# A new static order for a fused attention and convolution kernel: other costs and a deadline in the planner, fewer filler matmuls, one PSUM bank per convolution, six slots for output rows

## The chip, the core and the metric

The kernel runs on one core of a Trainium2 chip. The core has five engines that run their own instruction streams and meet only at semaphores: TensorE (PE, with its weight loads shown as PEld), VectorE (DVE), ScalarE (ACT), GpSimd (POOL) and SyncE (SP). The metric is the device time of one execution in microseconds. Three runs of the kernel before gave 596.65, 601.78 and 606.09 us; the median is 601.78 us.

## What is computed

Two independent layers are computed on inputs of 2048 rows by 448 columns, and a gate mixes them.

```python
def _A_ref(x, wq, wk, wv, wo):                      # 16 query heads share one key/value head
    q = (x @ wq).reshape(B, S, H, Dh).transpose(0, 2, 1, 3)      # S = 2048, D = 448, H = 16, Dh = 28
    k = x @ wk
    v = x @ wv
    p = softmax(einsum("bhqd,bkd->bhqk", q, k) * Dh ** -0.5)
    return einsum("bhqk,bkd->bhqd", p, v).transpose(0, 2, 1, 3).reshape(B, S, H * Dh) @ wo

def _B_ref(u, A_re, A_im, B_re, B_im, C_re, C_im, log_dt, Dskip):
    K[d, l] = Re sum_n C[d, n] * exp(dt[d] * A[d, n] * l) * dt[d] * B[d, n]   # N = 256, l < 2048
    return causal_convolution(u, K) + u * Dskip                  # one kernel per channel d

g = sigmoid((x * gate_w).sum(-1))
out = g * _A_ref(x, ...) + (1 - g) * _B_ref(x, ...)
```

## The kernel before

**Attention.** The scores are made as 1024 tiles of 128 keys by 512 queries (four heads, sixteen key blocks, sixteen groups of queries and heads). A QK set makes three or two tiles in one go, by turns, into one half of the buffer `psS` (line 1077; operation `mm` in `qk`). One ACT instruction takes the exponential of the whole set into `expT` (line 1093). A PV step multiplies four such tiles by the values, two sets behind, and accumulates in `psB` (line 1102); a column of ones gives the softmax denominators. After 64 tiles `norm` copies `psB` to `acc` (line 992), sends the denominators through DRAM and back (POOL's DMAs `denT`, `R_scratch`, `rdenB`) and writes the normalised rows to `onT`, a ring of four slots. `outp` multiplies four slots by `Wo`, `fold` adds the result, times the gate, to the output tile `O`.

**State space part.** The channels go in fourteen blocks `c` of 32. `masters` (DVE) squares powers for two or four blocks at a time, `tables` (DVE) expands them to the two factors of the convolution kernel, `kgen` (PE, line 894: 16 operations of 8 matmuls) multiplies these, and POOL writes the result to `KP_scratch` in DRAM in nine DMAs. `tload` reads it back as Toeplitz tiles `T`: 112 loads of 1072 KB, issued by SP into a ring of five slots. `conv` (two for each block, each on four `T` tiles) runs 8 operations of 4 matmuls for a tile (line 938) into one PSUM bank, DVE scales the bank to `cst` (line 947), PE transposes it (`yt`, line 958) into a second bank, and DVE adds that to `O` (line 966).

**The order.** Nothing is decided at run time. `Prog.schedule` is a list scheduler over all operations: each has an assumed duration, a priority `pr` (smaller goes first) and dependencies, and the one that could start earliest on its engine is placed next. Two PSUM banks (`POOL = (7, 5)`) are handed out as locks to everything but attention. The result is a fixed instruction list for each engine; each engine works its list strictly in order.

**Fillers.** Afterwards `fill` (line 587) walks the PE list and puts matmuls of zeros (lines 599, 602, 606) into every stretch in which the plan leaves PE idle, for three quarters of that stretch at an assumed 54 ns each:

```python
room = start - e0 - (pg.SWITCH if m0 != o.mode else 0.0) - 40.0
n = int(room * self.FILL / 54.0)
```

A filler of the kind of line 606 is four matmuls on the four column groups of the array, one of line 599 is a single matmul on 32 rows. They add zeros to `psB`, or write a bank that is not in use yet.

## Time and profile before

| | us |
|---|---|
| median of three runs (lowest, highest) | 601.78 (596.65, 606.09) |
| the profiled execution, its own time | 595.78 |
| its span, first to last instruction | 594.0 |
| PE busy, with 11359 matmuls | 514.2 |
| PEld busy, with 11374 weight loads | 302.4 |
| ACT busy | 489.5 |
| DVE busy | 461.8 |
| POOL busy | 140.2 |
| mean granted TensorE clock, as a share of full | 0.902 |

The profile shows one execution. Its page gives busy times, a chain of waits that ended last, and groups of instructions with the idle time ahead of them and what ended it. "issue" there is time in which an engine waited for nothing that the profile shows. Views of a stretch (busy time, waits, DMA queues, the timeline) use microseconds from the start of the span. In the profile a matmul's bar is longer than the pitch at which matmuls follow each other, so busy PE time is not work at peak.

### The profile page before, as it was taken

How to read it: one execution, taken by the hardware profiler on the slowest of the kernel's cores; microseconds unless marked ns; L12 is line 12 of the kernel's file. 1: busy time of each engine (PE TensorE's matmuls, PEld its weight loads, DVE VectorE, ACT ScalarE, POOL GpSimd, SP SyncE). 2: the span in 40 equal slices, each digit the busy share in tenths (PEclk: the TensorE clock that was granted, in tenths of full speed). 3: DMA queues.
4: the chain of work that ended last, by engine and by line, in shares of the span. 5: the costliest groups of instructions: out<-in, count | busy, mean ns of one | idle time of the engine just before them, and what ended most of it. 6: DMA issues, size and time to landing. Idle time of an engine off the chain costs nothing.

```text
span 594.0 us, 24569 instructions
## 1 busy us (share of the span) xinstructions
PE 514.2 (87%) x11359; PEld 302.4 (51%) x11374; DVE 461.8 (78%) x870; ACT 489.5 (82%) x427; POOL 140.2 (24%) x281
## 2 busy tenths in 40 slices
PE   7689898789899998798798998988998988968892
PEld 6445464445545455445455545645554545645552
DVE  6959997969979999979689899889597989100122
ACT  3669979879789999879689999888797999977750
POOL 2000114104124424231131523131141432412000
PEclk9858959979889999979789999989798999987896
DMA  8822001965926948968947847978838836597974
GB/s 244 230 106 74 2 20 31 400 223 167 391 71 190 411 136 315 380 219 347 380 167 272 274 184 264 402 259 311 313 120 357 336 144 229 213 383 284 357 260 169
DMA packets 36302, 143.11 MB, mean 241 GB/s; under 512 B 8880, under 2 KB 19224, under 8 KB 21864
## 3 DMA queue, kind: packets, MB, share of 16 engines
q1 hardware_dynamic: 27320, 135.29, 61.4%
q0 software_dynamic: 8352, 6.09, 4.3%
q8 instruction: 89, 1.46, 1.0%
q10 hardware_dynamic: 528, 0.17, 0.2%
q14 instruction: 13, 0.11, 0.1%
HBM read 135.38 MB, written 5.74 MB: 238 GB/s over the span
## 4 chain that ended last, share of the span: by engine, by line
PE 48%; DVE 23%; ACT 15%; issue 8%; DMA 3%; POOL 0%; ACTq 0%; another core or an unknown queue 0%
ACT expT L1093 15%; PE psS L1077 14%; PE psB L1102 9%; PE psS L938 6%; PE psB L606 5%; PE psX L894 4%; PE psX L938 3%; DVE tab L855 3%; DVE tab L861 2%; DVE tmp L857 2%; DVE tab L857 2%; DVE tab L859 1%; PE psS L894 1%; PE psB L599 1%; DMA sz<-in_gate_w_dram 1%
## 5 line engine op out<-in xcount | busy, mean ns | idle before, releaser
L1093 ACT ACTIVATE expT<-psS 128x1536 bf16<-128x1536 f32 (+1 forms) x410 | 474.6, 1261 | 70.7 <-PE psS L1077 68.4
L1077 PE MATMUL psS<-qT,kT 29*128 29x512 bf16 x1024 | 176.1, 416 | 15.7 <-ACT expT L1093 8.6
L1102 PE MATMUL psB<-expT,vaug 128*32 128x512 bf16 x1024 | 110.6, 421 | 5.5 <-issue 3.0
L129 POOL DMA_DIRECT2D KP_scratch<-kstg x126 | 67.5, 543 | 118.1 <-DVE kstg L907 115.5
L606 PE MATMUL psB<-ident,zero 128*32 128x128 bf16 x2672 | 71.8, 236 | 10.6 <-issue 10.5
L1077 PEld LDWEIGHTS psS<-qT,kT 29*128 29x128 bf16 x1024 | 41.5, 93 | 73.4 <-ACT expT L1093 37.5
L938 PE MATMUL psS<-T,U 128*24 128x128 bf16 (+7 forms) x2048 | 58.4, 248 | 13.4 <-issue 13.0
L855 DVE TENSOR_TENSOR tab<-tab,mbf 128x256 bf16<-128x256 bf16 (+4 forms) x70 | 68.6, 982 | 1.0
L606 PEld LDWEIGHTS psB<-ident,zero 128*32 128x32 bf16 x2672 | 55.4, 105 | 26.5 <-issue 18.2
L1102 PEld LDWEIGHTS psB<-expT,vaug 128*32 128x32 bf16 x1024 | 26.7, 94 | 74.2 <-issue 69.2
L938 PEld LDWEIGHTS psS<-T,U 128*24 128x24 bf16 (+7 forms) x2048 | 49.8, 162 | 25.6 <-issue 22.9
L129 POOL DMA_DIRECT2D denT<-acc x60 | 30.3, 511 | 135.0 <-DVE acc L992 133.1
L947 DVE TENSOR_TENSOR cst<-psS,omq 128x512 bf16<-128x512 f32 x16 | 11.0, 688 | 46.7 <-PE psS L938 46.6
L938 PE MATMUL psX<-T,U 128*20 128x128 bf16 (+7 forms) x1536 | 41.4, 241 | 5.2 <-issue 4.5
L129 POOL DMA_DIRECT2D rdenB<-R_scratch x60 | 30.4, 513 | 60.0 <-DMA R_scratch<-denT 59.9
L894 PE MATMUL psX<-tab 128*32 128x64 bf16 x1024 | 40.1, 290 | 3.5 <-issue 3.2
L938 PEld LDWEIGHTS psX<-T,U 128*20 128x20 bf16 (+7 forms) x1536 | 36.0, 163 | 13.4 <-issue 11.1
L894 PEld LDWEIGHTS psX<-tab 128*32 128x32 bf16 x1024 | 29.4, 137 | 13.9 <-issue 11.5
L857 DVE TENSOR_TENSOR tmp<-tab,mbf 128x256 bf16<-128x256 bf16 (+3 forms) x56 | 36.3, 649 | 0.0
L599 PE MATMUL psB<-ident,zero 32*128 32x128 bf16 x401 | 32.6, 230 | 1.5 <-issue 1.5
L872 DVE TENSOR_TENSOR tab<-tab,tmp 128x4096 bf16<-128x4096 bf16 x14 | 32.0, 2289 | 0.2
L857 DVE TENSOR_TENSOR tab<-tab,mbf 128x4096 bf16<-128x4096 bf16 x14 | 32.0, 2284 | 0.0
(149 smaller groups left out, 571.5 us busy)
## 6 DMA issues: line engine op xcount, KB each, us to landing
T<-KP_scratch SPq DMA_DIRECT2D x112, 1072.0 KB, 9.7
rdenB<-R_scratch POOLq DMA_DIRECT2D x60, 64.0 KB, 5.2
U<-in_A_x_dram SPq DMA_DIRECT2D x3, 896.0 KB, 14.7
tab<-in_A_x_dram SPq DMA_DIRECT2D x4, 448.0 KB, 7.2
KP_scratch<-kstg POOLq DMA_DIRECT2D x112, 16.0 KB
SZ_scratch<-tab SPq DMA_DIRECT2D x1, 1344.0 KB, 6.1
out_dram<-O SPq DMA_DIRECT2D x3, 448.0 KB, 3.8
sz<-SZ_scratch SPq DMA_DIRECT2D x3, 384.0 KB, 10.4
```

What stands on the lines that cost most here:

```text
L129: return [e.dma_start(o, i, **kw) for o, i in pairs]
L599: r = e.matmul(t.v(0, P, bo, [[1, 128]]), self.zero.v(0, 32, 0, [[1, P]]), self.ident.v(0, 32, 0, [[1, P]]), start=not acc, stop=False, ti ...
L606: r = e.matmul(t.v(32 * j, 32, bo, [[1, 128]]), self.zero.v(0, P, 0, [[1, 32]]), self.ident.v(0, P, 0, [[1, P]]), start=not acc, stop=Fals ...
L855: vo(lambda e, dst=dst, src=src, mr=mr: e.tensor_tensor(dst, src, mr, ALU.mult), 2 * n, done + mk(lv), [kr, ki])
L857: vo(lambda e, src=src, mi=mi, w=w, tb=tb, to=to: e.tensor_tensor(tb.v(0, P, to, [[w * EW, 2], [EW, w], [1, EW]]), src, mi, ALU.mult), 2 * ...
L861: vo(lambda e, do=do, n=n, tb=tb, to=to: e.tensor_tensor(tab.v(0, P, do + BLK, [[1, n]]), tab.v(0, P, do + BLK, [[1, n]]), tb.v(0, P, to, ...
L872: vo(lambda e: e.tensor_tensor(tab.v(0, P, FM, [[64, 2], [EW, 32], [1, 64]]), tab.v(0, P, lo + 31 * EW, [[BLK, 2], [-EW, 32], [1, 64]]), r ...
L894: r = e.matmul(G.v(32 * g, 32, 64 * jj, [[1, 64]]), tab.v(0, P, lo + comp * BLK + 64 + o, [[EW, 32]]), tab.v(0, P, fo, [[mo - fo, 2], [EW, ...
L938: r = e.matmul(ps.v(32 * j, 32 - 2 * n, 128 * k, [[1, 128]]), self.U.v(0, P, 2 * n * D + 4 * gi + j, [[D, 32 - 2 * n]]), self.T.v(0, P, s ...
L1077: r = e.matmul(self.psS.v(0, P, 512 * (bo + k), [[1, 512]]), kT.v(32 * h, DH + 1, 128 * kt, [[1, 128]]), qT.v(32 * h, DH + 1, 512 * (i % 2 ...
L1093: pg.op("act", lambda e: e.activation(expT.v(0, P, 512 * es, [[1, n]]), self.psS.v(0, P, 512 * bo, [[1, n]]), AF.Exp, scale=SQ), 100 + n / ...
L1102: r = e.matmul(self.psB.v(32 * h, 32, 0, [[1, 512]]), vaug.v(0, P, 32 * kt, [[1, 32]]), expT.v(0, P, 512 * (t % RING), [[1, 512]]), start= ...
```

## The change

**Costs in the planner.** A QK set's exponential is assumed at 50 ns plus its elements, where it was 100 ns plus those. A convolution operation is assumed at 94 to 57 ns, by its place in the tile, where all had 58; a `kgen` operation at 226 for 235, a `yt` operation at 75 for 85. A new field `st` holds the time that an operation streams through the array.

**A deadline.** While a QK set is ready, the scheduler works out when it must start so that ACT does not run dry by the plan (`dead`), and places no other PE operation of lower priority that would end later than that.

**Priorities and banks.** Convolution operations go from priority 4 to 1.8, transposes from 3.5 to 1.3. The transposes write the convolution's own bank, so that one lock is held instead of two. `cst` has two slots, `onT` six. The masters are squared in place in `sz` (`mst` and `qst` are gone), so a reload of `sz` waits for the last of the block before.

**Fillers.** `fill` now counts, for eight windows of 3413 ns around each idle stretch, how much streaming the plan has in them, and fills only up to a share of 0.55, at an assumed pitch of 90 ns. The PE list has 1378 filler matmuls where it had 3140; all else keeps its count.

```diff
+    MARGIN = 120.0
...
+            dead, busy = None, free["act"]
+            for i in ready["act"]:
+                busy = max(busy, rt[i]) + ops[i].ns
+            for i in ready["pe"]:
+                o = ops[i]
+                if o.mode == "q":
+                    dead = max(rt[i], busy - o.lat - self.SEM_NS - o.ns - self.MARGIN)
...
+                    if e == "pe" and o.mode != "q" and dead is not None and o.pr > 0:
+                        g = r + (0.0 if o.mode == mode else self.SWITCH) + o.ns + self.SWITCH
+                        if g > dead:
+                            continue
...
+def on(i):
+    return i % NON
...
-    FILL = 0.75
+    FILL = 90.0
+    WIN = 3413.0
+    SHARE = 0.55
...
-        self.onT = sb("onT", 4 * 512, BF)
+        self.onT = sb("onT", NON * 512, BF)
...
-            room = start - e0 - (pg.SWITCH if m0 != o.mode else 0.0) - 40.0
-            n = int(room * self.FILL / 54.0)
-            if n > 0 and (opened or k < used):
+            room = start - e0 - (pg.SWITCH if m0 != o.mode else 0.0) - 60.0
+            need = 0.0
+            if room > self.FILL and (opened or k < used):
+                for w0 in range(8):
+                    a = e0 - self.WIN * w0 / 8.0
+                    got = sum(max(0.0, min(a + self.WIN, u + d) - max(a, u)) for u, d in act if a - 400.0 < u < a + self.WIN)
+                    need = max(need, self.SHARE * self.WIN - got)
+            n = int(min(room, need * self.FILL / 54.0) / self.FILL)
+            if n > 0:
                 mode = m0 if m0 in ("c", "f") else o.mode if o.mode in ("c", "f", "q") else "q"
                 out.append(filler(n, mode, 6 if opened else 5, opened))
+                act.append((e0, 54.0 * n))
...
-        mst, msq, msr, mbf = self.mst, self.msq, self.msr, self.mbf
+        mst, msq, msr, mbf = self.sz, self.msq, self.msr, self.mbf
...
-                pg.op("pe", lambda e, mm=mm, comp=comp: mm(e, comp), 235, mode="c", rd=keys,
+                pg.op("pe", lambda e, mm=mm, comp=comp: mm(e, comp), 226, mode="c", st=54.0, rd=keys,
...
-        ps, px = self.grp(), self.grp()
+        co, ck = 512 * (c % 2), ("cst", c % 2)
+        ps = self.grp()
+        for k in range(4):
+            self.tload(4 * c + k)
...
-                pg.op("pe", mm, 58, mode="c", rd=[("T", s)] + [("U", q) for q in range(3)],
-                      wr=[X] + (["cst"] if first else []), pr=4,
+                pg.op("pe", mm, (94, 92, 90, 82, 76, 70, 58, 57)[n], st=54.0, mode="c", rd=[("T", s)] + [("U", q) for q in range(3)],
+                      wr=[X] + ([ck] if first else []), pr=1.8,
                       lock=ps if first else None)
...
-            pg.op("pe", lambda e, k=k: yt(e, k), 85, mode="h", rd=["cst", "id"], wr=[Y], pr=3.5, lock=px if k == 0 else None)
+            pg.op("pe", lambda e, k=k: yt(e, k), 75, st=40.0, mode="h", rd=[ck, "id"], wr=[Y], pr=1.3)
...
-                                                AF.Exp, scale=SQ), 100 + n / 1.2, rd=bk, wr=ew, pr=0)
+                                                AF.Exp, scale=SQ), 50 + n / 1.2, rd=bk, wr=ew, pr=0)
```

**What it moves on PE: a convolution among attention.** This is PE's list before, between the third and the fourth `T` tile of the first convolution (`L938` with `T,U` is the convolution, `L1077` a QK set, `L1102` a PV step, `L606` fillers).

```order
L938 MATMUL psS<-T,U 18x128 x4
L606 MATMUL psB<-ident,zero 32x128 x4
L1077 MATMUL psS<-qT,kT 128x512 x2
L1102 MATMUL psB<-expT,vaug 32x512 x4
L606 MATMUL psB<-ident,zero 32x128 x36
L1077 MATMUL psS<-qT,kT 128x512 x3
L1102 MATMUL psB<-expT,vaug 32x512 x4
L938 MATMUL psS<-T,U 32x128 x4
```

This is the same place in the changed list, where `L963` is the convolution, `L1102` a QK set, `L1127` a PV step and `L624` fillers.

```order
L963 MATMUL psS<-T,U 18x128 x4
L624 MATMUL psB<-ident,zero 32x128 x20
L1102 MATMUL psS<-qT,kT 128x512 x3
L1127 MATMUL psB<-expT,vaug 32x512 x4
L963 MATMUL psS<-T,U 32x128 x4
```

Between the two tiles stand 20 filler matmuls where 40 stood, and one QK set where two stood.

**What it moves on PE: the end.** This is PE's list before, from the last PV step of all on (`L1042` is the last output product, `L1009` and `L1020` are the two steps of the last normalisation, `L938` is the third `T` tile of the last convolution but one).

```order
L1102 MATMUL psB<-expT,vaug 32x512 x4
L1042 MATMUL psS<-Wo,onT 128x448 x3
L938 MATMUL psX<-T,U 30x128 x4
L938 MATMUL psX<-T,U 28x128 x4
L938 MATMUL psX<-T,U 26x128 x4
L1009 MATMUL psS<-msq,acc 128x4 x4
L938 MATMUL psX<-T,U 24x128 x4
L938 MATMUL psX<-T,U 22x128 x4
L938 MATMUL psX<-T,U 20x128 x4
L938 MATMUL psX<-T,U 18x128 x4
```

This is the same place in the changed list (`L1067` is the last output product, `L1034` and `L1045` the two steps of the normalisation, `L963` the same third tile).

```order
L1127 MATMUL psB<-expT,vaug 32x512 x4
L1067 MATMUL psS<-Wo,onT 128x448 x6
L1034 MATMUL psS<-msq,acc 128x4 x4
L1067 MATMUL psS<-Wo,onT 128x448 x6
L963 MATMUL psX<-T,U 32x128 x4
L1045 MATMUL psS<-msq,rdenB 128x128 x4
L963 MATMUL psX<-T,U 30x128 x4
L963 MATMUL psX<-T,U 28x128 x4
L963 MATMUL psX<-T,U 26x128 x4
L963 MATMUL psX<-T,U 24x128 x4
L963 MATMUL psX<-T,U 22x128 x4
L963 MATMUL psX<-T,U 20x128 x4
```

The third tile now follows twelve output products and both steps of the normalisation, where it stood around the first step and after three products.

More of the change, by code (lines that the diff above doesn't have):

```diff
@@ L32 @@
 RING = 15
+NON = 6
 KW = 1088
@@ L70 @@
     __slots__ = ("i", "eng", "fn", "ns", "lat", "deps", "pr", "lock", "unlock", "slot", "ndma",
-                 "count", "vc", "end", "comm", "extra", "mode")
+                 "count", "vc", "end", "comm", "extra", "mode", "st")
 class Prog:
@@ L96, in op @@
         o.mode = mode
+        o.st = st or (ns if eng == "pe" else 0.0)
         o.lat = self.LAT[eng] if lat is None else lat
@@ L615, in filler @@
             return o.i
+        act = [(o.end - o.lat - o.ns, o.st) for o in (pg.ops[x] for x in order) if o.st > 0]
         for k, x in enumerate(order):
@@ L975, in outp @@
             pg.op("pe", lambda e, g=g: e.matmul(
-                px(), self.onT.v(0, P, g * 512 + 128 * tt, [[1, 128]]), self.Wo.v(0, P, g * D, [[1, D]]),
+                px(), self.onT.v(0, P, on(4 * qc + g) * 512 + 128 * tt, [[1, 128]]), self.Wo.v(0, P, g * D, [[1, D]]),
                 start=(g == 0), stop=(g == 3), tile_position=(0, 0), skip_group_check=True), 200,
-                rd=["Wo"] + [("on", gg) for gg in range(4)], wr=[X], pr=2, lock=G if g == 0 else None)
+                rd=["Wo"] + [("on", on(4 * qc + gg)) for gg in range(4)], wr=[X], pr=2, lock=G if g == 0 else None)
         self.fold(qc, tt, px, 0, D, [X], unlock=G)
```

54 lines of the change are left out of this document (24 added, 30 removed).

## Prediction

> **What bounds the kernel now.** I read the page first, then busy time by stretch, then who waited for whom in the long middle stretch. The page:
>
> ```profile
> span 594.0 us, 24569 instructions
> PE 514.2 (87%) x11359; PEld 302.4 (51%) x11374; DVE 461.8 (78%) x870; ACT 489.5 (82%) x427; POOL 140.2 (24%) x281
> q8 instruction: 89, 1.46, 1.0%
> L1093 ACT ACTIVATE expT<-psS 128x1536 bf16<-128x1536 f32 (+1 forms) x410 | 474.6, 1261 | 70.7 <-PE psS L1077 68.4
> ```
>
> The exponentials alone take 474.6 us, 0.4635 us for each of the 1024 tiles. They cannot overlap each other, so nothing below about 475 us plus a head and a tail is possible. ACT sat idle 70.7 us ahead of them, nearly all of it for a QK set. The chain of waits around 48 us shows the pace when nothing is missing: 21 in 24.06 us, 1.146 us each.
>
> ```profile
> 47.89 24.06 ACT expT L1093 x21
> ```
>
> By stretch (columns: length; busy time and instructions of PE, PEld, DVE, ACT, POOL; granted clock; DMA share; GB/s):
>
> ```profile
> 36.50:48.00 11.50, 11.50 (x137) 6.20 (x137) 8.35 (x12) 8.28 (x9) 0.00 (x0) 0.50 0.01 1
> 48.00:71.80 23.80, 20.21 (x408) 11.67 (x405) 23.16 (x78) 23.80 (x22) 2.14 (x4) 1.00 0.16 47
> 71.80:88.90 17.10, 16.90 (x267) 9.90 (x267) 16.86 (x33) 13.25 (x13) 2.54 (x5) 0.50 0.07 18
> 100.00:572.50 472.50, 419.12 (x9839) 241.76 (x9852) 370.88 (x673) 414.42 (x358) 127.63 (x244) 0.93 0.74 272
> 572.50:594.00 21.50, 10.29 (x254) 7.49 (x250) 6.94 (x12) 0.00 (x0) 0.00 (x0) 0.76 0.60 213
> ```
>
> The loss is in the middle: from 100 to 572.5 ACT is idle 472.50 - 414.42 = 58.1 us. Then 21.5 us of tail follow in which it has no work. In the middle, ACT waits for QK sets, and PE, which should make them, itself waits for nothing that the profile shows:
>
> ```profile
> ACT expT L1093 <- PE psS L1077: 56.1, 63, 3.2
> PE psS L938 <- issue: 13.0, 8, 3.3
> PE psB L606 <- issue: 10.5, 8, 2.2
> PE psX L894 <- issue: 3.2, 3, 1.7
> PE psX L938 <- issue: 3.2, 5, 2.0
> PE psB L1102 <- issue: 3.0, 2, 1.6
> PE psS L1077 <- issue: 2.5, 3, 2.0
> ```
>
> These six rows make 35.4 us in 29 waits, in convolutions, fillers, `kgen` and attention alike, so it is not the work at hand that stops PE. The DMA queues of that stretch show what does:
>
> ```profile
> q1 hardware_dynamic: 17087, 121.11, 67.9%
> q8 instruction: 76, 1.25, 1.0%
> ```
>
> The instruction queue moved 76 packets. Over the whole run it moved 89, and PE has 11359 + 11374 = 22733 instructions, 255 for each packet: the packets are PE's instructions, 256 at a time. 472.5 / 76 makes 6.2 us for a block of 256, while q1, with the `T` tiles, fills 68% of the engines. From 117.26 to 121.25 one block ran; the columns are start, length, engine, line, operation, count and the idle time ahead:
>
> ```profile
> 117.26 0.34 PE L606 MATMUL psB<-ident,zero 128*32 128x128 bf16 x9 [1.69 <-issue]
> 124.28 0.32 PE L938 MATMUL psS<-T,U 128*18 128x128 bf16 x3 [2.78 <-issue]
> ```
>
> PE came out of one issue wait at 117.26, and stood in the next from 121.5. Its matmuls in between, by group:
>
> ```profile
> L938 PE MATMUL psS<-T,U 128*32 128x128 bf16 (+7 forms) x60 | 1.7, 238 | 0.0
> L1077 PE MATMUL psS<-qT,kT 29*128 29x512 bf16 x10 | 1.6, 385 | 0.0
> L606 PE MATMUL psB<-ident,zero 128*32 128x128 bf16 x49 | 1.3, 220 | 1.7 <-issue 1.7
> L1102 PE MATMUL psB<-expT,vaug 128*32 128x512 bf16 x8 | 0.8, 390 | 0.0
> ```
>
> That is 127 matmuls and as many weight loads, one block. PE used it up in 4 us and got the next one 7.0 us after the last. **So PE starves for instructions wherever it runs through 256 of them in less than some 6 us**, and 49 of these 127 were fillers. What follows costs more:
>
> ```profile
> 117.26:124.28 7.02, 4.24 (x130) 2.71 (x130) 2.96 (x9) 4.62 (x4) 2.12 (x4) 0.91 1.04 377
> 124.28:129.84 5.56, 5.56 (x109) 3.02 (x109) 5.20 (x15) 3.31 (x3) 0.00 (x0) 0.50 0.68 241
> ```
>
> After the wait the clock is at half, and ACT is busy 3.31 of 5.56 us. Where blocks are spread evenly, none of this happens:
>
> ```profile
> 167.40:230.00 62.60, 60.10 (x1316) 32.30 (x1306) 59.60 (x104) 60.27 (x54) 23.65 (x45) 1.00 0.58 201
> ```
>
> 2622 instructions in 62.6 us are 6.1 us a block, the clock is full, and ACT loses 2.33 us, 3.7%.
>
> The Trainium skill, "Runtime: NRT & Kernel Launch", section "Instruction fetch mechanics", says that an engine's instructions come in blocks of 16 KiB, 256 instructions, over a DMA queue of its own, and that crossing a block is mostly hidden. The trace agrees on the block; on the hiding it does not, in this stretch.
>
> **The change, part by part.**
>
> *Fewer fillers.* In the middle stretch stand these:
>
> ```profile
> L606 PE MATMUL psB<-ident,zero 128*32 128x128 bf16 x2228 | 58.8, 231 | 10.6 <-issue 10.5
> L599 PE MATMUL psB<-ident,zero 32*128 32x128 bf16 x241 | 18.7, 220 | 1.5 <-issue 1.5
> ```
>
> That is 2469. The changed list has 959 from the same tile on (tile 128 of 1024), 1510 fewer; with their loads 3020 instructions, 11.8 blocks. 76 blocks become 64. At 6.2 us each these need 397 us, less than ACT's 414.4: on average fetching no longer binds. Locally it still can. I cut each PE list into pieces of 128 matmuls and gave each piece 0.4635 us for every QK tile in it, which is how long ACT takes over them. Where that is under the time of a fetch, the difference is lost. With 5.5 us for a fetch the list before loses 54 to 61 us, depending on where the cutting starts, and the changed one 12 to 17; with 6.2 it is 90 to 100, and 28 to 36. The measured 58.1 us is near the first pair. So ACT's idle time in the middle goes from 58.1 to between 12 and 36 by this count; the even stretch above, at 3.7%, would make it 17. I take 26, on the upper side, for the half clock that fewer fillers may bring and for `T` tiles that PE may now reach sooner. **That is -32**, with a best of -44 (3% left) and a worst of -12, if only the issue waits that now stand in fillers (10.5 and 1.5) go.
>
> *The deadline and the pitches.* They keep a QK set from queueing behind convolution work. In the even stretch, where nothing else disturbs, that is worth no more than its 2.33 us; over the middle 3.7% is 17 us at most, and it is inside the bounds above. The rule adds no wait on the chip, since it only chooses an order. Its cost would be convolutions that pile up for the end; the changed list has 224 convolution matmuls after the last QK set, against 192. I take nothing for that beyond the tail below.
>
> *Early part, 36 to 100 us.* ACT lost 3.2 us of 11.5 and 3.85 of 17.1 at half clock, and nothing at full clock. Fillers there go from 661 to 419 over the first 128 tiles. At half clock fewer of them stand ahead of a QK set, which saves up to half of these 7 us; if the half clock (22% lost) held over all 63.5 us, it would cost 7 more. I take +1, with 13 fewer of the fillers ahead of the first transposes in it.
>
> *The tail.* What ends the run is the last `T` load, which waits for the third tile of the last convolution but one:
>
> ```profile
> 574.51 1.05 PE L1009 MATMUL psS<-msq,acc 128*128 128x4 f32 x8
> 576.48 1.16 PE L1020 MATMUL psS<-msq,rdenB 128*128 128x128 f32 x8
> 576.01 5.89 DMA T<-KP_scratch
> 571.53 0.74 PE L1042 MATMUL psS<-Wo,onT 128*128 128x448 bf16 x3
> ```
>
> In the changed list nine more output products (0.22 us each by the last row) and the second step (1.16) stand ahead of that tile: 2.0 + 1.2 = 3.2 us, less the 0.4 that the tile's own operations now follow without a break. **+3**; between 0, if the products still run while PE waits for ACT, and 6 with one more issue wait.
>
> *The rest.* One bank for the convolution and its transposes, six slots in `onT`, two in `cst`: PE waited for none of these in the rows above, so I take 0. Squaring in place in `sz` delays three reloads on SP's queue behind the block before, with `T` loads queued behind them; they are placed where the plan has them ready, 0 to 10 us each if the plan is late, and I take 0.
>
> *The sum:* 594.0 - 32 + 1 + 3 = 566.0. The profiled execution's own time is 1.8 above its span, so 567.8. It was the fastest of all the runs shown, 6 us below their median. I expect less spread when the issue waits go, and **forecast 570 us**, with a range of its own from 554 to 586.
>
> **Rivals.**
>
> *The clock falls, slower.* Fillers keep the array busy; without them the clock could stay at half. For it: the stretches at half clock are among those with most fillers in the list, and there 661 go to 419. Against it:
>
> ```profile
> 345.50:353.00 7.50, 7.50 (x164) 4.44 (x164) 7.36 (x22) 7.50 (x8) 2.55 (x5) 1.00 0.43 163
> 68.40:71.80 3.40, 2.92 (x57) 2.06 (x53) 3.40 (x5) 3.40 (x4) 2.06 (x4) 1.00 0.03 2
> L599 PE MATMUL psB<-ident,zero 32*128 32x128 bf16 x30 | 2.0, 215 | 0.0
> L606 PE MATMUL psB<-ident,zero 128*32 128x128 bf16 x12 | 0.3, 219 | 0.0
> ```
>
> In the first window there is not one filler, and the clock stayed full. In the second 42 of 57 matmuls are fillers, there is no issue wait, and half clock followed at 71.8 all the same. Price: at half clock ACT loses 22% (13.25 busy of 17.10). With a share h of the middle at half clock it takes 414.4 / (1 - 0.03 - 0.225 h); today h is 0.14, by the clock of 0.93. At h = 0.38 the gain is gone, from 0.5 it is slower by 2%, and at 0.6 it is 414.4 / 0.835 = 496, 24 more than now: **about 624**. Chance 0.06; a half-way house, h about 0.35, at 590 to 602: 0.11.
>
> The Trainium skill, "TensorE: Matmul & The Clock Gate", section "Why this matters for your kernels", asks for no idle gap of PE over about 3 us to keep the clock. By that rule the changed kernel would keep it, and the issue waits alone lose it. The second window above disagrees: its clock fell without such a gap.
>
> *The fetch is not the cause.* If blocks are late for another reason, the issue waits (35.4) stay, and only the remaining 58.1 - 35.4 = 23 us can shrink, to the 17 of the even stretch: 594.0 - 6 + 4 + 1.8 = **594**. For it, fetches are only 1% of DMA time; against it, the wait after 117.26 came exactly at a block's end. Chance 0.10. The skill's "mostly hidden", above, is this case.
>
> *Another bound comes up.* DVE works 461.8 us, and `T` loads move 121 MB; PE faster by 5% may wait for either in its fixed order. If half of the 32 us is lost to that: **584**. Chance 0.11. The DMA share of 0.74 in the middle leaves a quarter, which speaks against more.
>
> **How the numbers follow.** The forecast holds 0.62, and the others 0.06, 0.11, 0.10 and 0.11 as said. About 2%, 12 us, is what a measurement of this kernel can tell from no change, so faster is below 589.7. All of the forecast, the last rival and a third of the fetch case lie there: 0.62 + 0.11 + 0.04 = 0.77. Slower is the clock rival, 0.05 of its 0.06; the rest, 0.18, is within 2%. The range runs from 552, the best of the middle and tail, to 597, which leaves out the clock's worse half and the forecast's ends.
>
> **What would show it.** In the changed profile the instruction queue has about 75 packets; PE's issue waits in the middle fall from 35 to below 15 us; the clock there rises from 0.93 to about 0.96; ACT's idle time ahead of its exponentials falls from 70.7 to about 40; the last stretch without ACT is near 24 us. I am wrong if the packets fall and the issue waits stay, or if both fall and the clock falls too.

## The result, and the profile after

The changed kernel takes **565.4 us** (median of four runs, 559.59 to 570.59), the kernel before 599.2 us in the runs beside it (591.75 to 606.09). The ratio is 0.948, with an interval from 0.932 to 0.965. This ratio and those of the table below leave out the runs that lie more than 1.5% above the fastest of their kernel, so they are not the quotients of the medians. The forecast was 570 us, with a range from 552 to 597.

The profiled execution of the changed kernel took 570.59 us, 5.2 above the median, at a mean clock of 0.860; that of the kernel before took 595.78, 3.4 below its median, at 0.902. So the profiles show a gain of 25.2 us where the medians show 33.8.

The page of the changed kernel:

```profile
span 568.8 us, 21055 instructions
PE 509.4 (90%) x9612; PEld 277.1 (49%) x9612; DVE 462.6 (81%) x870; ACT 486.5 (86%) x427; POOL 140.4 (25%) x281
q8 instruction: 75, 1.23, 0.8%
L1118 ACT ACTIVATE expT<-psS 128x1536 bf16<-128x1536 f32 (+1 forms) x410 | 471.6, 1291 | 41.5 <-PE psS L1102 35.0
```

75 packets of instructions instead of 89, and 41.5 us of idle time ahead of the exponentials instead of 70.7. By stretch (length; busy time and instructions of PE, PEld, DVE, ACT, POOL; granted clock; DMA share; GB/s), where the second ends with the last exponential:

```profile
36.50:100.00 63.50, 63.21 (x789) 30.91 (x788) 52.74 (x128) 56.77 (x50) 6.08 (x12) 0.57 0.08 23
100.00:540.34 440.34, 405.14 (x8322) 216.37 (x8326) 374.52 (x680) 411.08 (x359) 130.90 (x250) 0.92 0.78 287
540.34:568.80 28.46, 16.62 (x280) 11.52 (x268) 7.53 (x13) 0.00 (x1) 0.00 (x0) 0.62 0.60 221
```

The first of these stretches in the kernel before, which the prediction did not show:

```profile
36.50:100.00 63.50, 59.40 (x1019) 33.22 (x1020) 56.26 (x137) 56.43 (x51) 9.16 (x18) 0.78 0.10 25
```

In the middle ACT is idle 440.34 - 411.08 = 29.3 us (58.1 before). The tail is 28.46 us (21.50 before). The clock fell in the early stretch from 0.78 to 0.57, was 0.92 in the middle (0.93 before), and 0.62 in the tail (0.76 before). PE's waits in the middle for which the profile shows no releaser (total, times, longest):

```profile
PE psX L963 <- issue: 2.8, 4, 1.2
PE psX L917 <- issue: 2.7, 3, 1.4
PE psB L1127 <- issue: 1.9, 2, 1.3
PE psS L917 <- issue: 0.9, 1, 0.9
PE psS L963 <- issue: 0.6, 1, 0.6
PE psX L983 <- issue: 0.3, 1, 0.3
```

They make 9.2 us in 12 waits, all shorter than 1.5 us. Before there were 38.4 us in 32 waits (35.4 in the six rows that the prediction shows, and three small rows), up to 3.3 us long. What ACT waited for in the changed kernel's middle:

```profile
ACT expT L1118 <- PE psS L1102: 24.2, 41, 1.6
ACT expT L1118 <- PE psB L1127: 4.4, 2, 3.4
```

The second row is new: two exponentials waited for a PV step to free their slots in `expT`.

### The profile page after: what moved, and what is told of

It reads as the page before. It is cut to its first block, busy times and chain, and to the rows that moved or that the text cites. A ratio compares the mean times of both kernels' runs of the same rounds, so it can differ in the third digit from the quotient of the medians.

```text
span 568.8 us, 21055 instructions
## 1 busy us (share of the span) xinstructions
PE 509.4 (90%) x9612; PEld 277.1 (49%) x9612; DVE 462.6 (81%) x870; ACT 486.5 (86%) x427; POOL 140.4 (25%) x281
## 4 chain that ended last, share of the span: by engine, by line
PE 36%; ACT 22%; DVE 18%; DMA 17%; issue 3%; POOL 3%; ACTq 0%
ACT expT L1118 22%; PE psS L1102 11%; PE psB L1127 7%; DMA denT<-acc 6%; DMA T<-KP_scratch 4%; DMA rdenB<-R_scratch 3%; PE psB L617 2%; PE psB L624 2%; DMA R_scratch<-denT 2%; PE psX L963 2%; DVE tab L878 2%; DVE tab L880 2%; PE psS L917 2%; PE psX L917 2%; DVE tab L882 2%
## 5 line engine op out<-in xcount | busy, mean ns | idle before, releaser
L1118 ACT ACTIVATE expT<-psS 128x1536 bf16<-128x1536 f32 (+1 forms) x410 | 471.6, 1291 | 41.5 <-PE psS L1102 35.0
L1102 PE MATMUL psS<-qT,kT 29*128 29x512 bf16 x1024 | 183.4, 433 | 13.9 <-ACT expT L1118 10.0
L1127 PE MATMUL psB<-expT,vaug 128*32 128x512 bf16 x1024 | 113.8, 435 | 3.6 <-issue 1.9
L1102 PEld LDWEIGHTS psS<-qT,kT 29*128 29x128 bf16 x1024 | 42.4, 93 | 84.6 <-ACT expT L1118 48.7
L1127 PEld LDWEIGHTS psB<-expT,vaug 128*32 128x32 bf16 x1024 | 26.8, 95 | 72.5 <-issue 69.3
L963 PE MATMUL psX<-T,U 128*18 128x128 bf16 (+7 forms) x1920 | 54.9, 246 | 3.7 <-issue 2.8
L963 PEld LDWEIGHTS psX<-T,U 128*18 128x18 bf16 (+7 forms) x1920 | 46.6, 162 | 19.2 <-issue 15.3
L963 PE MATMUL psS<-T,U 128*32 128x128 bf16 (+7 forms) x1664 | 49.9, 246 | 6.2 <-DMA T<-KP_scratch 4.7
L963 PEld LDWEIGHTS psS<-T,U 128*26 128x26 bf16 (+7 forms) x1664 | 42.9, 161 | 17.5 <-issue 8.0
L917 PE MATMUL psX<-tab 128*32 128x64 bf16 x896 | 36.0, 289 | 2.8 <-issue 2.7
L624 PE MATMUL psB<-ident,zero 128*32 128x128 bf16 x1112 | 36.9, 259 | 0.1
L917 PE MATMUL psS<-tab 128*32 128x64 bf16 x896 | 34.7, 289 | 0.9 <-issue 0.9
L624 PEld LDWEIGHTS psB<-ident,zero 128*32 128x32 bf16 x1112 | 26.5, 114 | 12.9 <-issue 10.9
L917 PEld LDWEIGHTS psS<-tab 128*32 128x32 bf16 x896 | 26.1, 137 | 9.3 <-issue 7.2
## 6 DMA issues: line engine op xcount, KB each, us to landing
U<-in_A_x_dram SPq DMA_DIRECT2D x3, 896.0 KB, 15.9
```

The lines of the kernel that those rows point to most:

```text
L624: r = e.matmul(t.v(32 * j, 32, bo, [[1, 128]]), self.zero.v(0, P, 0, [[1, 32]]), self.ident.v(0, P, 0, [[1, P]]), start=not acc, stop=Fals ...
L917: r = e.matmul(G.v(32 * g, 32, 64 * jj, [[1, 64]]), tab.v(0, P, lo + comp * BLK + 64 + o, [[EW, 32]]), tab.v(0, P, fo, [[mo - fo, 2], [EW, ...
L963: r = e.matmul(ps.v(32 * j, 32 - 2 * n, 128 * k, [[1, 128]]), self.U.v(0, P, 2 * n * D + 4 * gi + j, [[D, 32 - 2 * n]]), self.T.v(0, P, s ...
L1102: r = e.matmul(self.psS.v(0, P, 512 * (bo + k), [[1, 512]]), kT.v(32 * h, DH + 1, 128 * kt, [[1, 128]]), qT.v(32 * h, DH + 1, 512 * (i % 2 ...
L1118: pg.op("act", lambda e: e.activation(expT.v(0, P, 512 * es, [[1, n]]), self.psS.v(0, P, 512 * bo, [[1, n]]), AF.Exp, scale=SQ), 50 + n / ...
L1127: r = e.matmul(self.psB.v(32 * h, 32, 0, [[1, 512]]), vaug.v(0, P, 32 * kt, [[1, 32]]), expT.v(0, P, 512 * (t % RING), [[1, 512]]), start= ...
```

## The experiments

The question was what the 29 us in the middle are made of (fewer instructions to fetch, less filler time on PE, or the new order), why the clock did not rise as forecast, and why the tail grew by 7 us and not by 3. "Middle" is from 100 us to the last exponential. "Issue" is the total of PE's issue waits there, "idle" ACT's idle time there, "clock" the granted clock there; the packets are those of the whole run, the tail is behind the last exponential. All but the first two columns come from each kernel's one profiled execution; those of e4 and e7 lay 8 and 17 us above their medians. Each ratio is taken to runs of the kernel before that were made beside that experiment; their medians lay between 597.9 and 602.1 us.

| kernel | median us | ratio to before, interval | packets | issue | idle | clock | tail |
|---|---|---|---|---|---|---|---|
| before | 599.2 | 1 | 89 | 38.4 | 58.1 | 0.93 | 21.5 |
| changed | 565.4 | 0.948 (0.932 to 0.965) | 75 | 9.2 | 29.3 | 0.92 | 28.5 |
| e1 before, new filler rule | 586.9 | 0.979 (0.970 to 0.988) | 81 | 25.1 | 49.7 | 0.92 | 21.7 |
| e2 changed, old filler rule | 571.6 | 0.958 (0.951 to 0.965) | 80 | 13.1 | 36.6 | 0.92 | 24.1 |
| e3 before, wide fillers | 572.9 | 0.961 (0.954 to 0.968) | 77 | 15.9 | 38.9 | 0.95 | 21.4 |
| e4 changed, no fillers behind tile 128 | 562.7 | 0.941 (0.933 to 0.949) | 67 | 0.8 | 27.5 | 0.86 | 29.2 |
| e5 before, no fillers behind tile 128 | 567.8 | 0.953 (0.947 to 0.959) | 69 | 2.8 | 34.1 | 0.85 | 21.8 |
| e6 before, light `T` loads | 548.2 | 0.919 (0.910 to 0.928) | 89 | 4.0 | 16.3 | 0.97 | 18.8 |
| e7 changed, old rule, wide fillers | 564.3 | 0.946 (0.938 to 0.955) | 72 | 8.3 | 33.8 | 0.91 | 30.7 |
| e8 changed, no deadline | 559.1 | no interval | 75 | 8.8 | 30.5 | 0.92 | 21.8 |
| e9 changed, last tile earlier | 565.1 | 0.943 (0.933 to 0.953) | 75 | 9.3 | 28.6 | 0.93 | 22.6 |
| e10 before, `T` loads in four pieces | 597.5 | 0.991 (0.985 to 0.997) | 89 | 30.7 | 60.0 | 0.93 | 21.0 |
| e11 changed, no deadline, old rule, wide | 554.8 | 0.926 (0.919 to 0.934) | 71 | 6.3 | 25.9 | 0.94 | 18.7 |
| e12 changed, light `T` loads | 535.7 | 0.898 (0.889 to 0.907) | 75 | 2.2 | 6.8 | 0.97 | 22.4 |

### e1: the new filler rule alone

```diff
-    FILL = 0.75
+    FILL = 90.0
+    WIN = 3413.0
+    SHARE = 0.55
...
(in fill, the counting of the changed kernel; kgen and conv with st=54.0, yt with st=40.0)
```

> The kernel before with only the new filler rule (windows of 3413 ns, share 0.55, pitch 90 ns); the old costs, priorities, banks, and no deadline. Fillers from tile 128 on: 1644, where the kernel before has 2479 and the changed one 959. Theory F (PE starves for instructions, 256 at a time): the list cut into pieces of 128 matmuls, 5.5 us for each piece and 0.4635 us for each QK tile in it, loses 28 to 34 us in the middle, where the list before loses 54 to 61 and the changed one 12 to 17 by the same count. So about half to two thirds of the whole gain of 34 us: 572 to 578 us against 599, PE's issue waits in the middle near 18 us (35.4 before, 9.2 in the changed kernel). Theory O (the gain is the new order: deadline, pitches, priorities): no gain, within 2% of 599, whatever the issue waits do.

Measured: 586.9 us, 2% less than before, where theory F had 572 to 578. Issue waits fell to 25.1 us, not as far as the 18 that F asked for. So the rule alone carries some two fifths of the gain (2.1 of 5.2%; with these intervals only a rough share), and F's count is too hopeful: 49.7 us idle where it had 28 to 34. A part of what is missing lies in the plan, that is, in the order and times that the scheduler works out before fillers go in: in the old plan this rule makes 1644 fillers behind tile 128, in the new plan 959.

### e2: the new plan with the old filler rule

```diff
-    FILL = 90.0
-    WIN = 3413.0
-    SHARE = 0.55
+    FILL = 0.75
...
-            n = int(min(room, need * self.FILL / 54.0) / self.FILL)
+            n = int(room * self.FILL / 54.0)
...
```

> The changed kernel with the old filler rule (three quarters of every idle stretch at 54 ns each); its costs, deadline, priorities and banks stay. Because the new costs leave less idle time in the plan, the old rule now makes 1417 fillers from tile 128 on (959 with the new rule, 2479 in the kernel before). Theory F: 19 to 26 us lost in the middle by the count with 5.5 us a piece, where the changed list has 12 to 17: 8 us slower than the changed kernel, 573 us, with issue waits near 15 us. Theory O: the same time as the changed kernel, 565 us. If the fillers hold the clock up (the clock theory), it is as fast or faster than the changed kernel, with a clock in the middle above 0.92.

Measured: 571.6 us, near the 573 of F, with 13.1 us of issue waits and the clock at 0.92, not above; the intervals of this kernel and of the changed one overlap. The old rule in the new plan makes 1417 fillers behind tile 128; in the old plan it made 2479. So **the new plan by itself takes away more fillers (1062) than the new rule does in the old plan (835)**. The likely reason is that a plan with longer assumed convolution operations has less idle time to fill, but costs, deadline, priorities and banks are new here together and were not told apart. The prediction counted these fillers as gone; it did not see that the plan, and not only the rule, removes them.

### e3: the same filler time in a quarter of the instructions

```diff
+                def one(c):
+                    mv = self.ident.v(0, P, 0, [[0, c], [1, P]]) if c > 1 else self.ident.v(0, P, 0, [[1, P]])
...
+                    for j in range(4):
+                        r = e.matmul(t.v(32 * j, 32, bo, [[1, P * c]]), self.zero.v(0, P, 0, [[1, 32]]), mv,
+                                     start=not acc, stop=False, tile_position=(0, 32 * j), skip_group_check=True)
...
-                for _ in range(n):
+                for _ in range(n // 4):
+                    r = one(4)
+                for _ in range(n % 4):
+                    r = one(1)
```

> The kernel before with the same filler time in a quarter of the instructions: every four fillers of 128 columns (four times 52 to 54 ns) become one of 512 columns. The order, the real work and the time that PE spends on fillers stay; 1315 filler matmuls are left from tile 128 on, where 2479 were. Theory F: issue waits in the middle fall from 35.4 to about 15 us, and by the count (17 to 31 us lost) the time falls by about 30 us, to 570, with the clock of the middle at 0.93 or above. If it is the time of the fillers on PE that counts, or their place ahead of QK sets, not the number of instructions: no change, within 2% of 599.

Measured: 572.9 us, with issue waits of 15.9 us. The middle of this kernel (the groups, and the stretch):

```profile
L1099 ACT ACTIVATE expT<-psS 128x1536 bf16<-128x1536 f32 x356 | 411.1, 1267 | 38.9 <-PE psS L1083 37.5
100.00:549.38 449.38, 416.90 (x8663) 220.06 (x8662) 368.96 (x668) 410.44 (x356) 125.54 (x240) 0.95 0.77 284
```

The order is that of the kernel before, PE spends about the same time on fillers in the middle (83.3 us of matmuls, 78.3 before), and 3.9% of the time is gone. So most of what these fillers cost is their number of instructions, not their time on PE nor their place in the list. That it is the fetching, e6 shows below: it keeps every filler and its weight load.

### e4 and e5: no fillers behind tile 128, in either order

```diff
...
-            if n > 0:
+            if n > 0 and done < 32:
...
             if pv is not None:
+                done += 1
                 opened = pv < 15
```

This is the edit of e4; `done` counts PV steps, of four tiles each. e5 puts the same condition into the kernel before.

> The changed kernel without any filler behind tile 128 of 1024 (959 fewer matmuls, 7.5 blocks of 256 instructions less). Theory F alone: 6 to 12 us lost in the middle instead of 12 to 17, issue waits below 4 us: about 560 us. The clock theory: without fillers the share h of the middle at half clock goes up; at half clock ACT lost 22% early on. The changed kernel has 0.92 there (h of 0.16); with h of 0.5 it would be 0.225 x 0.34 x 445 = 34 us slower, 599 us. Which of the two is larger tells what the fillers that are left are worth.

> The kernel before with no filler behind tile 128 of 1024; the old order and costs stay. From there on PE has as many instructions as the changed kernel without its fillers there had (59.7 blocks of 256), so the two differ by the order alone. Theory F (the block count sets the time, the order is worth little): ACT idle in the middle near 30 us (27.5 there, 58.1 before), issue waits below 5 us, about 565 us. Theory O (deadline, pitches and priorities carry the gain): no better than the kernel before with the new filler rule alone, 580 us or more, with ACT waiting for QK sets 45 us or more in the middle although the issue waits are gone.

Measured: 562.7 us in the new order (the changed kernel: 565.4; the intervals overlap), 567.8 in the old one. Both have the same number of instructions left there, and hardly an issue wait. The rows of the old order without fillers:

```profile
L1094 ACT ACTIVATE expT<-psS 128x1024 bf16<-128x1024 f32 x357 | 411.7, 1267 | 34.1 <-PE psS L1078 32.8
100.00:545.00 445.00, 402.84 (x7369) 200.08 (x7366) 368.86 (x670) 410.91 (x357) 126.63 (x242) 0.85 0.77 287
```

The middle of e4:

```profile
100.00:539.97 439.97, 404.22 (x7376) 198.14 (x7372) 374.85 (x681) 412.44 (x360) 131.50 (x251) 0.86 0.77 287
```

Two things follow. Taking out every filler of the middle gives 24.0 us of idle time (58.1 to 34.1) in the old order, with the clock down to 0.85; in this comparison the new order is worth 34.1 - 27.5 = 6.6 us of idle time. And the fillers that the changed kernel keeps there buy nothing that shows: without them the clock falls from 0.92 to 0.86, the issue waits go, and the idle time stays (29.3 and 27.5). The clock theory's 599 us did not come.

### e6 and e12: the same instructions, light T loads

```diff
-        pg.dma([(self.T.v(0, P, s * TW, [[1, TW]]),
-                 dram(self.KP, 4 * gi * KW, [[1, 64], [KH, 2], [1, TW]]))],
+        src = [[1, 64], [KH, 2], [1, TW]] if gi < NTR else [[1, 32], [1, TW]]
+        pg.dma([(self.T.v(0, P if gi < NTR else 32, s * TW, [[1, TW]]), dram(self.KP, 4 * gi * KW, src))],
```

This is the edit of e6; e12 makes the same one in the changed kernel. From the sixth load on only 32 of the 128 partitions of a tile are written, a quarter of the bytes. The convolutions then work on stale rows and the output is not the right one; every instruction is still there.

> The kernel before, all 2479 fillers kept, with the loads of T cut from the sixth on: 32 partitions of 128 are written, the others keep what the first five loads left (the convolutions behind them compute with stale rows). The order and the number of instructions stay. Theory F as the prediction put it (a block takes 6.2 us because T loads fill the DMA engines): issue waits in the middle fall from 35.4 us to below 10, and the time to 570 or below. If a block takes its time whatever the DMA engines carry, the issue waits stay above 25 us and the time above 588.

> The changed kernel with the loads of T cut from the sixth on to 32 partitions of 128 (the convolutions behind them compute with stale rows); its order and instructions stay. The kernel before, cut in the same way, took 548.2 us with 16.3 us of idle time on ACT in the middle. If the change gains by the fetch alone, nothing of its gain is left when the fetch is not short: 546 to 552 us, the same as the kernel before so cut, at 16 us of idle time in the middle, or a little slower by its tail and its clock. If the order gains by itself (5 us by the two runs without fillers): 540 us or below, 12 us idle or less. If the 29 us that the changed kernel still loses have another cause than the T loads, ACT stays idle for 25 us or more: 560 us.

Measured: 548.2 us for the kernel before so cut, 535.7 for the changed one. The kernel before, light loads (instruction queue of the whole run; the middle; its issue waits, all of them):

```profile
q8 instruction: 89, 1.46, 1.2%
100.00:527.36 427.36, 408.07 (x9856) 236.06 (x9853) 369.57 (x674) 411.01 (x359) 127.62 (x245) 0.97 0.40 100
PE psB L606 <- issue: 3.4, 4, 2.0
PE psX L894 <- issue: 0.6, 1, 0.6
```

Every filler is still there, 89 packets are fetched as before, in the same order; only the DMA share fell from 0.74 to 0.40, and 34 of 38 us of issue waits are gone. **A block of instructions is late because `T` loads fill the DMA engines.** The clock went up with it, from 0.93 to 0.97, without a filler added. The changed kernel, light loads:

```profile
L1118 ACT ACTIVATE expT<-psS 128x1024 bf16<-128x1024 f32 x357 | 404.6, 1402 | 6.8 <-PE psS L1102 4.1 <-PE psB L1127 2.5
100.00:510.64 410.64, 384.78 (x8305) 212.07 (x8314) 370.13 (x678) 403.80 (x357) 127.43 (x244) 0.97 0.40 103
```

6.8 us idle, where the kernel before has 16.3 under the same light loads and at the same clock. So 9.5 us of idle time go when the fetch is hardly short. They are not the order's alone, since the changed kernel also has fewer fillers and 2.2 us of issue waits for 4.0; between the two kernels without fillers, which differ by the order alone, it was 6.6. And 22.5 of the 29.3 us that the changed kernel still loses hang on the `T` loads, though its issue waits are only 9.2. How they divide was not tried: with light loads the clock is higher too, and other transfers land sooner (`rdenB` in 2.6 us by the median, where it took 5.5).

### e7, e8, e11: wide fillers and no deadline in the changed kernel

```diff
-                    if e == "pe" and o.mode != "q" and dead is not None and o.pr > 0:
+                    if e == "pe" and o.mode != "q" and dead is not None and o.pr > 99:
```

This is the edit of e8. e7 puts e3's wide fillers and the old rule into the changed kernel, e11 puts both together.

> The changed kernel with the old filler rule, every four of its fillers made one of 512 columns: the filler time of the run with the old rule in the changed kernel (571.6 us) in 715 filler matmuls from tile 128 on instead of 1417. Theory F: 65.3 blocks from there on, ACT idle in the middle 29 us as in the changed kernel (29.3 at 67.2 blocks) or less. With the clock held up by the filler time (0.85 instead of 0.57 between 36 and 100 us in the run with the old rule) the early stretch gains 3 us and the tail, at full clock, 4: about 558 us. If fillers as such cost PE time that QK sets need, it is no faster than 571.

> The changed kernel with the deadline taken out of the scheduler; costs, priorities, banks and the filler rule stay. It has 903 fillers from tile 128 on (959), 66.7 blocks for 67.2, so the fetch hardly differs. If the deadline is worth nothing beyond 2 us (the prediction): 563 to 567 us, ACT idle in the middle 27 to 32. If the deadline carries a part of the gain: 575 us or more, ACT waiting for QK sets 40 us or more in the middle, in waits that end with a convolution ahead of the QK set.

> The changed kernel without the deadline, with the old filler rule, and every four fillers made one of 512 columns: 64.9 blocks from tile 128 on, 160 convolution matmuls behind the last QK set (224). What the earlier runs showed apart, put together: the fetch as in the changed kernel (issue waits 8 us), a tail of 22 us instead of 28, and a clock of 0.9 or above. About 556 us, if the gains add up; 564, as with the wide fillers and the deadline, if the deadline's absence is worth nothing.

Measured: e7 564.3 us, no better than the changed kernel, though better than e2 with the same filler time in small pieces (571.6; the intervals just touch). The early stretch did not get the full clock back in its profiled execution (0.53), so the gain of 7 us forecast for clock and tail did not come. e8 559.1 us, below the 563 to 567 that were expected, but its runs go from 545.54 to 563.67, too wide for an interval; its quickest run had a mean clock of 0.937, its slowest 0.867. ACT's idle time in the middle, 30.5, is that of the changed kernel (29.3): in the middle the deadline is worth nothing that shows. In the tail it costs: without it 160 convolution matmuls stand behind the last QK set, with it 224. The tail is 21.8 us at a clock of 0.79 there, where e2, with the deadline and a clock of 0.78, has 24.1.

e11 takes **554.8 us** (551.58 to 558.01; 556 were expected), 0.926 of the kernel before, and 554.8 / 565.4 = 0.981 of the changed kernel's median. By its median it is the quickest version found that does all of the work; its interval just touches that of the changed kernel. Its tail and its middle:

```profile
534.08:552.81 18.73, 9.49 (x227) 7.02 (x225) 6.93 (x12) 0.00 (x0) 0.00 (x0) 0.88 0.60 221
L1114 ACT ACTIVATE expT<-psS 128x1536 bf16<-128x1536 f32 x358 | 409.4, 1315 | 25.9 <-PE psS L1098 19.5 <-PE psB L1123 4.2 <-PE psB L617 1.3
```

### e9: the third tile ahead of half of the products

```diff
-                      wr=[X] + ([ck] if first else []), pr=1.8,
+                      wr=[X] + ([ck] if first else []), pr=0.3 if c >= 26 else 1.8,
```

> The changed kernel with the last two convolutions at priority 0.3 (1.8): on PE the third tile of the last convolution but one now follows six of the twelve output products and only the first of the two normalisation steps, and the fourth tile follows it; nothing else moves. If the last T load, which waits for that tile, ends the run (the prediction's step for the tail): the tail behind the last exponential falls from 28.4 us by 3 us or more. If the tail is PE's own work at half clock, one after the other (the products took 0.41 us each there, 0.22 before): the tail stays at 27 to 29 us at half clock, and 24 at full, and the time is that of the changed kernel, 565 us.

Measured: 565.1 us, the changed kernel's time, and a tail of 22.6 us at a clock of 0.88. The changed kernel's tail on PE (start, length, line, operation, count, idle time ahead):

```profile
542.29 2.42 PE L1067 MATMUL psS<-Wo,onT 128*128 128x448 bf16 x6 [1.06 <-DVE onT L1026]
544.51 1.71 PE L1034 MATMUL psS<-msq,acc 128*128 128x4 f32 x8
546.08 2.40 PE L1067 MATMUL psS<-Wo,onT 128*128 128x448 bf16 x6
548.69 2.08 PE L1045 MATMUL psS<-msq,rdenB 128*128 128x128 f32 x8
554.69 0.45 PE L983 MATMUL psX<-ident,cst 128*64 128x64 bf16 x16 [1.11 <-DVE cst L972]
556.00 3.55 PE L963 MATMUL psS<-T,U 128*32 128x128 bf16 x128 [0.87 <-DVE O L1009]
```

Six products take 2.42 us, 0.40 each (0.25 before, 0.74 for three), and the second step of the normalisation 2.08 (1.16 before): half clock. The last convolution waits for DVE, which folds the last output product out of the bank that it needs, and not for a `T` load. The `T` load is close behind, though: SP issued the last one at 551.7, behind the third tile, and it took 5.4 us to land, so it landed at 557.1, after this convolution had begun and some 1.4 us before its fourth tile was due. The first row also shows how the tail begins: PE waits 1.06 us for `onT`, which waits for the softmax denominators on their way through DRAM. In the chain that ended last (start, length):

```profile
518.29 7.49 DMA denT<-acc
526.35 5.84 DMA R_scratch<-denT
533.95 7.58 DMA rdenB<-R_scratch
541.54 0.70 DVE onT L1026
```

In e4 and e7 this wait is 3.70 and 2.46 us long, and their tails (29.2 and 30.7 us) are longer by it. The same list of PE from the first product on in e2, where the clock was 0.78 there, makes a tail of 24.1, with no wait for `onT`. In e9 the `T` load is back as the last releaser:

```profile
540.99 1.31 PE L1067 MATMUL psS<-Wo,onT 128*128 128x448 bf16 x6 [1.22 <-DVE onT L1026]
544.36 1.05 PE L1045 MATMUL psS<-msq,rdenB 128*128 128x128 f32 x8
551.91 0.81 PE L963 MATMUL psX<-T,U 128*32 128x128 bf16 x32 [0.65 <-DMA T<-KP_scratch]
```

So of the 7 us by which the tail grew, 24.1 - 21.5 = 2.6 come with the order and 28.5 - 24.1 = 4.4 with the clock; the move of the tile itself is worth at most about 1.5 (24.1 to 22.6, where the clock is higher too), less than the 3 that the first theory asked for. In e9 the last convolution also got another bank (`psX` for `psS`), so not the tile alone moved. These are single profiled executions at three clocks, so the halves are only rough.

### e10: the T loads in four pieces

```diff
...
+        h = TW // 4
-        pg.dma([(self.T.v(0, P, s * TW, [[1, TW]]),
-                 dram(self.KP, 4 * gi * KW, [[1, 64], [KH, 2], [1, TW]]))],
+        pg.dma([(self.T.v(0, P, s * TW + h * z, [[1, h]]),
+                 dram(self.KP, 4 * gi * KW + h * z, [[1, 64], [KH, 2], [1, h]])) for z in range(4)],
```

> The kernel before with each T load written as four loads of a quarter of the columns: packets of 2144 bytes for 8576, the same bytes, the same order on every engine. If a block of instructions waits behind the packets of T that stand in front of it, and each now holds an engine a quarter as long: issue waits in the middle fall from 36 to 15 us or less and the time to 575 or below. If the wait goes by the bytes in front of it, not by the packets, the issue waits and the time stay (30 us or more, 592 or more).

Measured: 597.5 us, 0.9% less, with 30.7 us of issue waits and 60.0 us of idle time. So the size of the packets in front of a block is not what delays it, or hardly; the bytes are. e6, with a quarter of the bytes, is the other side of this. The middle of e10:

```profile
100.00:570.94 470.94, 418.68 (x9801) 239.03 (x9814) 368.22 (x668) 410.99 (x356) 125.00 (x239) 0.93 0.80 272
```

## Why the prediction was right, and where its steps were not

The total came out, from terms that were partly off:

| term, against the profiled executions | forecast | measured |
|---|---|---|
| ACT's idle time in the middle | -32 | 29.3 - 58.1 = -28.8 |
| the exponentials themselves | 0 | 471.6 - 474.6 = -3.0 |
| early stretch | +1 | 56.43 - 56.77 = -0.3 |
| tail | +3 | 28.46 - 21.50 = +7.0 |
| sum | -28 | -25.1 |

That the total is only 3 us off is partly luck: two terms brought 3.2 and 4.0 us less than forecast, and 4.3 us came where nothing or a loss was expected.

**PE starves for instructions.** Right. The packets fell to 75, as forecast, issue waits from 35 (38.4 with the small rows) to 9.2 (forecast: below 15), and three experiments that leave the order alone agree: fewer instructions at the same filler time (e3), no fillers (e5), and the same instructions with light `T` loads (e6). The rival that blocks are late for another reason is out. The Trainium skill, "Runtime: NRT & Kernel Launch", section "Instruction fetch mechanics", calls the crossing of a block mostly hidden; e6 shows when that holds here (4.0 us of issue waits at a DMA share of 0.40) and the kernel before when it does not (38.4 at 0.74).

**Fewer fillers: -32, of 58.1.** Nearly right in sum (-28.8), wrong in its working. The step fitted 5.5 us a block so that the count gave all 58.1 us of the kernel before to the fetch. But 16.3 us are left when the loads are light (e6), and in all the kernels with fewer instructions the idle time is 14 to 19 us above the middle of what the count with 5.5 gives: 29.3 against 12 to 17 in the changed kernel, 49.7 against 28 to 34 in e1, 36.6 against 19 to 26 in e2, 38.9 against 17 to 31 in e3, 27.5 against 6 to 12 in e4. Taking 26, above the count, made up for that; the prediction gave half clock and `T` tiles as its reasons, but no working for the size.

**The deadline and the pitches: no more than 2.33 us in the even stretch, 17 us at most over the middle.** The bound held, with 6.6 us for the order without fillers (e4, e5) and at most 9.5 with light loads (e6, e12). But the prediction gave the order no price of its own and put all of the -32 down to fewer instructions. Of the deadline and the pitches, the deadline brings nothing in the middle that shows, and costs in the tail (e8). So the order's gain comes from the costs (the pitches among them), priorities, banks and slots together; which of these was not tried. With the old rule the new plan alone takes away 1062 of the 1520 fillers that the change removes behind tile 128 (e2).

**The clock: from 0.93 to 0.96.** Wrong: 0.92, with issue waits down to a quarter, so these waits were not all that brought it down. Over the whole run the other three executions had 0.868 to 0.894, where the kernel before had 0.902 in its profile. Fillers do hold it up (0.86 and 0.85 without them), and the light loads do too (0.97 in both kernels). The early stretch shows how loosely the clock hangs on the list. It had 0.57 in the changed kernel and 0.74 in e12, whose PE list is the same:

```profile
36.50:100.00 63.50, 57.11 (x802) 27.23 (x803) 55.54 (x131) 58.78 (x52) 9.02 (x18) 0.74 0.09 24
```

The price of half clock, 22% of ACT's time, is not one number either. ACT's 56.77 us at 0.57 are only 2.0 less than these 58.78, and no less than the 56.43 before; but in e7, at 0.53, ACT was busy for only 51.77 us of this stretch. In the changed kernel's middle, up to its last exponentials, lie eight stretches at half clock; three of them and the sum of all eight:

```profile
101.90:118.96 17.06, 16.75 (x242) 8.32 (x242) 16.26 (x31) 15.37 (x14) 4.23 (x8) 0.50 0.80 299
388.62:398.86 10.24, 10.24 (x169) 4.83 (x173) 8.82 (x26) 8.69 (x8) 2.81 (x6) 0.50 0.30 96
412.51:422.75 10.24, 10.24 (x105) 3.23 (x105) 8.41 (x18) 8.70 (x8) 2.00 (x4) 0.50 1.01 415
sum 68.26, PE 67.30 PEld 29.44 DVE 57.86 ACT 55.71 POOL 16.78; mean PE 8.41 PEld 3.68 DVE 7.23 ACT 6.96 POOL 2.10
```

ACT loses 68.26 - 55.71 = 12.6 us there, 18%, not the 22% of the one stretch from which the rival was priced. So 12.6 of the 29.3 us that are left lie in stretches at half clock; that the clock causes all of them is not shown. The Trainium skill, "TensorE: Matmul & The Clock Gate", section "Why this matters for your kernels", asks that PE have no gap over some 3 us; here these are PE's longest waits in the middle (total, times, longest), and the clock fell eight times all the same:

```profile
PE psS L963 <- DMA T<-KP_scratch: 4.7, 5, 1.9
PE psB L1127 <- DVE acc L1017: 1.7, 1, 1.7
```

So keeping to the rule was not enough here.

**The tail: +3, because the last `T` load waits for a tile behind twelve products.** The size was off, 7.0, and the cause in part: the load did wait for that tile and was late, but it landed some 1.4 us before it was due, and the wait for the denominators, PE at half clock and the bank of the last convolution set the end (e9). The forecast bounds, 0 to 6, held no term for the clock. The 0.22 us for a product is also less than the row beside it gives (0.74 us for three, 0.25 each).

**The rest at 0.** Right within what can be seen, but for one new wait: 4.4 us in which exponentials waited for PV steps.

**The other rivals.** The falling clock had a price of 22% of the time at half clock; e4, with 0.86 in the middle, took 562.7 us, no more than the changed kernel with 0.92, and in its stretches at half clock ACT lost 14% (17.7 of 126.3 us). "Another bound" is there in part: 22.5 us of what is left hang on the `T` loads (e12), but half of the gain was not lost to it.

## What to carry to other kernels

Where an engine waits and nothing in the profile releases it, count its instructions against the packets of the instruction queue, and look at what else the DMA engines carry then: the same filler time in fewer, larger instructions (e3, 572.9 us) was worth nearly as much as leaving the fillers of the middle out (e5, 567.8). A change of a plan has a second effect wherever something is generated from the plan's gaps, so count what is generated before pricing the rule that generates it. And a model with one free number that explains all of a loss in one kernel should be tried against a kernel without the suspected cause before it prices a change.

## What was not expected of the hardware

The delay of a block of instructions goes with the bytes that the `T` loads move, hardly with the size of their packets: a quarter of the bytes took the issue waits from 38.4 to 4.0 us, a quarter of the packet size only to 30.7.

The granted clock differs from run to run of one program, and the time with it: the changed kernel's four runs took 570.6, 566.3, 564.5 and 559.6 us at mean clocks of 0.860, 0.868, 0.879 and 0.894, and e8's went from 563.7 at 0.867 to 545.5 at 0.937. That is some 3 us for 0.01 of clock in these two kernels, as much as several of the terms above. It is no fixed rule: of e9's runs one at 0.868 took 563.4 us and one at 0.888 took 566.5. What decides the clock was not found.
